# Gated attention and low-rank mixer on one core: the 64-row output tile on four array quadrants, the low-rank step and the burst order moved

## The chip, the cores and the metric

The kernel runs on one core of one Trainium2 chip. The metric is the time of one execution in microseconds (us) on the device, as the median of several runs; less is better. Verdicts are given at 2%: "faster" needs a ratio below 0.98.

Five engines matter. PE is TensorE, the matrix unit; PEld is its loading of weights; ACT is ScalarE; DVE is VectorE; POOL and SP mostly issue DMAs. Each has its own list of instructions in the program and waits for the others by semaphores (counters that one engine raises and another waits on); in the timelines below each works through its list in order.

## The reference

Eight batches, 3136 rows, 256 columns, keys of 64 columns:

```python
scores = (1 / S) * z @ z.T          # S = 3136, z: S x 64
attn   = maximum(scores, 0) ** 2
x      = u * (attn @ v)             # u, v: S x 256

h   = x.T @ U @ V                   # U: S x 32, V: 32 x S   (low rank)
y   = x + h.T
out = y + maximum(y @ w1, 0) @ w2   # w1: 256 x 1024, w2: 1024 x 256
```

## The kernel before

The 3136 rows make 25 tiles: 24 of 128 rows and one of 64 rows (tile `NF = 24`). For each batch the kernel computes 25 *outputs*, one row tile of `attn @ v` each, in the order 12, 13, ..., 24, 0, ..., 11. I number them 0 to 24 in that order, so the 64-row tile is output 12. Into the attention of batch b it weaves the mixer of batch b-1: a *rank* step after output 0 (`x.T @ U`), a *low-rank* step in seven outputs (one for each chunk of up to four tiles), and *bursts* of first-layer steps ("up") and second-layer steps ("down") after outputs 2, 4, 6, 8, 10, 13, 15, 17. It also fills in *scores* (z times z) for its own later outputs and for the next batch.

Each attention matmul takes 64 of 128 rows of the contraction, so two of them run side by side in the two row halves of the array, into two banks of PSUM, the memory that takes TensorE's sums; the pair of banks is summed when two outputs are done (`close_pair`). There are two sets of two banks. One accumulates; the other, `spare()`, serves the low-rank step and the second layer, once the pair before has been summed out of it.

Three inputs of the matmuls are transposed by DMA ("turned"): `zT` (z for the scores), a *strip* (blocks of attn) and `ut` (a chunk of x + h.T for the first layer). A score passes from PE to ACT (L273, the maximum) and to DVE (L275, the square).

```python
def attend_steps(b, o):                  # 25 steps of one output
    def step(i):
        ...
        if i < NT - 1:
            w = block(b, o, js[i])       # 128 x 128 block of attn
            half(b, o, js[i], 0, w, ...) # rows 0..63   -> bank 0
            half(b, o, js[i], 1, w, ...) # rows 64..127 -> bank 1
        ...
        if i == NT - 1 and o == last:
            close_pair(b, o)

def close_pair(b, o):
    nc.scalar.copy(out=both[:, :w], in_=banks[1][:, :w])                   # L347 ACT
    nc.vector.tensor_tensor(both[:, :w], banks[0][:, :w], both[:, :w], add)  # L348 DVE
    nc.vector.tensor_tensor(x_at(b, t0, n), both, u_sb, mult)              # L351 DVE

def low_rank(b, c, ps=None):
    ps = spare() if ps is None else ps
    for ...: mm(out=ps[h][...], lhsT=V_bf[...], rhs=t1[b][...])            # L421 PE
    for h in range(2):
        nc.vector.tensor_tensor(q, ps[h], q, add)                          # L435 DVE
    transpose(out=ut, in_=x)                                               # DMA, for the up steps

# the loop over outputs
main = attend_steps(b, o)
if b and i in ahead:                       # outputs 1, 2, 4, 6, 8, 10, 13
    main.insert(NT * 2 // 5, low_rank step)   # step 10 of 25
_spread(main, fill)                        # fill: score steps, evenly spread
...
run(_merge(down, up))                      # the burst; a down step also takes spare()
```

The 64-row output costs as many matmuls as any other: its rows are doubled into both halves of the 128 weight columns, and half of what comes out is a copy.

Of the kernel before, what the change touches and what calls it, by code (L numbers as in the profile page):

```python
# [10 lines left out]
ALU = mybir.AluOpType  # L11
# [3 lines left out]
def _ceil_div(a, b):  # L15
    return (a + b - 1) // b
# [15 lines left out]
def _merge(*lists):  # L32

    keyed = [
        ((i + 0.5) / len(part), n, s)
        for n, part in enumerate(lists)
        for i, s in enumerate(part)
    ]
    return [s for _, _, s in sorted(keyed, key=lambda e: e[:2])]
# [3 lines left out]
def kernel(  # L43
# [11 lines left out]
    nc = tc.nc  # L55

    B, S, D = u.shape
# [4 lines left out]
    NT = _ceil_div(S, P)  # L62
    NF = S // P
# [31 lines left out]
    halves = [slice(h * ROWS, (h + 1) * ROWS) for h in range(2)]  # L95
# [12 lines left out]
    mm = nc.tensor.matmul  # L108
# [9 lines left out]
    v_both = [persist.tile([P, NT, D], BF16, name=f"v{k}") for k in range(2)]  # L118
# [30 lines left out]
    def x_at(b, t, n=1):  # L149

        c, k = offset[t]
        return group(b, c)[:, :, k : k + n, :].rearrange("p a t c -> p t a c")

    def split(ap):
        return ap.rearrange("p (t a c) -> p t a c", a=ND, c=P)
# [148 lines left out]
    acc = {}  # L304
    u_tiles = {}

    def pair_of(o):
        first = 0 if o < FIRST else FIRST
        stop = FIRST if o < FIRST else NT
        t0 = o - (o - first) % 2  # L310
        return t0, min(2, stop - t0)
# [11 lines left out]
    def open_pair(b, o):  # L323
        acc[pair_of(o)[0]] = sets[opened[0] % 2]
        opened[0] += 1

    def block(b, o, j):
        k = (o - j) % NT
        return A[j][:, k * P : (k + 1) * P] if k <= HALF else strips[b, o][:, NT - 1 - k, :]

    def half(b, o, j, h, w, start, stop, **kw):
        t0, _ = pair_of(o)
        mm(  # L333
            out=acc[t0][h][:, (o - t0) * D : (o - t0 + 1) * D],
            lhsT=w[halves[h]],
            rhs=v_both[b % 2][halves[h], j, :],
            start=start,
            stop=stop,
            **kw,
        )  # L340

    def close_pair(b, o):
        t0, n = pair_of(o)
        banks, u_sb = acc.pop(t0), u_tiles.pop((b, t0))
        w = n * D
        both = both_pool.tile([P, 512], FP32, name="both")
        nc.scalar.copy(out=both[:, :w], in_=banks[1][:, :w])  # L347
        nc.vector.tensor_tensor(  # L348
            out=both[:, :w], in0=banks[0][:, :w], in1=both[:, :w], op=ALU.add
        )  # L350
        nc.vector.tensor_tensor(  # L351
            out=x_at(b, t0, n),
            in0=split(both[:, :w]),
            in1=u_sb[:, :n, :].rearrange("p t (a c) -> p t a c", c=P),
            op=ALU.mult,
        )

    def after(b, o):

        t0, n = pair_of(o)  # L360
        i = place(t0) + n
        return (b, turns(i)) if i < NT else (b + 1, turns(0))

    def attend_steps(b, o):
        t0, n = pair_of(o)
        last = t0 + n - 1
        js = [(o - k) % NT if k < NB else (o + k - HALF) % NT for k in range(NT)]
        js.remove(NF)

        def step(i):  # L370
            if i == 0 and o == t0:
                open_pair(b, o)
                if after(b, o)[0] < B:
                    load_u(*after(b, o))
            if i < NT - 1:
                w = block(b, o, js[i])
                end = i == NT - 2
                half(b, o, js[i], 0, w, i == 0, end and o > t0)
                half(b, o, js[i], 1, w, i == 0 and o == t0, end)
            elif o == t0:  # L380
                half(b, o, NF, 0, block(b, o, NF), False, True)
                if o < last:
                    half(b, o + 1, NF, 1, block(b, o + 1, NF), True, False)
            if i == NT - 1 and o == last:
                close_pair(b, o)

        return [lambda i=i: step(i) for i in range(NT)]
# [26 lines left out]
    def low_rank(b, c, ps=None):  # L414

        ts = chunks[c]
        ps = spare() if ps is None else ps
        where = [(0, 0), (1, 0)] if len(ts) == 2 else [(0, 0), (0, 1), (1, 0), (1, 1)]
        order = sorted(zip(where, ts), key=lambda e: (e[0][1], e[0][0]))
        for (h, k), t in order:  # L420
            mm(  # L421
                out=ps[h][:, k * D : (k + 1) * D],
                lhsT=V_bf[halves[h], col(t) : col(t) + P],
                rhs=t1[b][halves[h], :],
                start=True,
                stop=True,
            )
        n = len(ts)
        x = group(b, c)
        dst = x.rearrange("p a t c -> p t a c")  # L430
        for h in range(2):
            ks = [k for (g, k), _ in zip(where, ts) if g == h]
            k0 = len(ks) * h if n == 2 else 2 * h
            q = dst[:, k0 : k0 + len(ks)]
            nc.vector.tensor_tensor(out=q, in0=split(ps[h][:, : len(ks) * D]), in1=q, op=ALU.add)  # L435
        ut = ut_pool.tile([P, ND * 512], BF16, name="ut")
        ut = ut[:, : ND * n * P].rearrange("p (a w) -> p a w", a=ND)
        transpose(
            out=ut.rearrange("p a (t c) -> p (a t) c", c=P),
            in_=x.rearrange("p a t c -> p (a t c)"),  # L440
        )
        uT[c] = ut
# [211 lines left out]
    own_at = {i: [] for i in range(NT)}  # L654
    for i, j in enumerate(range(LEAD + NG - 1, NT)):
        own_at[i].append((j, 0, NB))
    for j, i in enumerate((6, 7, 8, 9, 10, 10, 4, 2, 9, 8, 7, 6)):
        own_at[i].append((j, 0, FIRST - j))


# [11 lines left out]
    def run(steps):  # L672
        for s in steps:
            s()
# [5 lines left out]
    for b in range(B):  # L680
        more = b + 1 < B
        begin = 0 if b else 2 * NG
        bursts = bursts_of(b - 1) if b else []
        burst_at = dict(zip((2, 4, 6, 8, 10, 13, 15, 17), range(NC + 1)))
        z_load, z_double, z_half, z_turn = (1, 5, 7, 11) if b else (None, 9, 11, 13)
        soon = next_at if b else next_first
        v_at = (1, 3, 4, 5, 7, 8, 10, 11, 12) if b else (8, 9, 10, 12, 14, 15, 16, 17, 18)
        v_at = dict(zip(v_at, V_PARTS))
        ahead = dict(zip((1, 2, 4, 6, 8, 10, 13), range(NC)))
        first = []  # L690
        if b == 0:
            for j, k1 in [(NT - 1, NB)] + [(j, NB if j < 3 else FIRST - j) for j in range(FIRST)]:
                first += score_steps(j, 0, k1)
        for i in range(begin, NT):
            o = turns(i)
            fill = []
            if b == 0:
                if i < z_turn:
                    n = _ceil_div(len(first), z_turn - i)
                    fill, first = first[:n], first[n:]  # L700
            else:
                fill = [s for key in own_at[i] for s in score_steps(*key)]
            if more:
                fill += [s for key in soon[i] for s in score_steps(*key)]
                if i == z_load:
                    load_z(b + 1, WHOLE)
                if i == z_double:
                    double_z(b + 1, WHOLE)
                if i == z_half:
                    turn_z(b + 1, ((FIRST, NF),))  # L710
                if i == z_turn:
                    turn_z(b + 1, ((0, FIRST),))
                if i == z_turn + 1:
                    extend_z()
                if i in v_at:
                    load_v(b + 1, v_at[i])
            main = attend_steps(b, o)
            if b and i in ahead:
                main.insert(NT * 2 // 5, lambda c=ahead[i]: low_rank(b - 1, c))
            _spread(main, fill)  # L720
            if i + AHEAD < NT:
                turn(b, turns(i + AHEAD))
            elif more:
                turn(b + 1, turns(i + AHEAD - NT))
            if b == 0 and i in weights:
                weights[i]()
            if b and i == 0:
                rank(b - 1)
            if b and i in burst_at:
                up, down = bursts[burst_at[i]]  # L730
                if not more and burst_at[i] >= NC - 1:
                    late += up + (down if burst_at[i] == NC else [])
                    up, down = [], (down if burst_at[i] < NC else [])
                run(_merge(down, up))


    last = bursts_of(B - 1)
# [5 lines left out]
    for c in range(NC + 1):  # L743
        up, down = last[c]
        if c + 2 < NC:
            up = up[:1] + [lambda c=c: low_rank(B - 1, c + 2, other)] + up[1:]
# [30 lines left out]
```

## Time and profile before

| | before |
|---|---|
| median of three runs | 1065.91 us (1064.72 to 1067.03) |
| PE busy | 1010.7 us, 95% |
| repeat, batches 2 to 5 | 126.8 us |
| attention matmul, start to start | 54.6 ns (two side by side) |
| output 12 (49 attention matmuls) | 2.68 us |

The page's first part, and the first lines of its part on the chain that ended last (shares of the span):

```profile
PE 1010.7 (95%) x13829; PEld 791.3 (74%) x13829; DVE 525.3 (49%) x937; ACT 611.4 (57%) x814; POOL 178.7 (17%) x332
...
PE 81%; DVE 7%; ACT 5%; issue 3%; DMA 2%; POOL 1%; SPq 0%; POOLq 0%; ACTq 0%; DVEq 0%
```

TensorE bounds this kernel. "Busy", though, hides short waits: the page counts a matmul busy from its start to a modelled end some 270 ns later, and in a stream the next starts 55 ns later. The Trainium skill ("Perfetto Trace Analysis", Tensor Engine Instruction) says the same: the start is taken when the operands are fetched, the end is computed. So I measure a wait on PE by starts: how much later a matmul starts than its stream's rate allows. By that measure output 4's low-rank matmul below is 0.58 us late; by the page's idle column it is 0.37.

The chain in order of time shows each batch's rank step; the columns are start, length, and what. The differences between such lines are the repeats:

```profile
496.98 1.53 PE ps L401 x50
623.82 1.53 PE ps L401 x50
```

The view of waits (who waited for whom: us in total, times, longest), three lines:

```profile
PE ps L260 <- DMA zT<-z_bf: 15.8, 2, 9.6
PE ps L421 <- DVE both L348: 8.3, 28, 0.4
PE ps L333 <- DVE x_bf L435: 2.3, 7, 0.3
```

The two waits for zT are in the start-up and in batch 0. The 28 of L421 are four in each of seven batches, at outputs 4, 6, 8 and 10. The timeline of output 4 (columns: start, length, engine, line, what, count, idle before) shows one:

```profile
513.35 0.58 ACT L347 COPY both<-ps 128x512 f32<-128x512 f32 x1
513.99 0.68 DVE L348 TENSOR_TENSOR both<-ps,both 128x512 f32<-128x512 f32 x1
514.73 0.40 PE L421 MATMUL ps<-t_sb,V_bf 64*128 64x256 bf16 x4 [0.37 <-DVE both L348]
515.82 1.28 DVE L435 TENSOR_TENSOR x_bf<-ps,x_bf 128x512 bf16<-128x512 f32 x2
517.16 0.38 PE L486 MATMUL ps<-w_bf,relu 128*128 128x256 bf16 x2
```

PE comes to the low-rank step while DVE still sums the pair before out of the same banks (L348 ends at 514.67). The burst then begins with a second-layer step (L486) at 517.16, just after the low-rank adds L435 have left its bank (515.82 + 1.28 = 517.10).

Output 12 in the timeline, its first 24 and the next 24 of 49 matmuls:

```profile
566.49 1.47 PE L333 MATMUL ps<-v,A 64*128 64x256 bf16 x24
567.80 1.47 PE L333 MATMUL ps<-v,strip 64*128 64x256 bf16 x24
```

567.80 - 566.49 = 1.31 us for 24 starts, 54.6 ns each.

### The profile page before, as it was taken

How to read it: one execution, taken by the hardware profiler on the slowest of the kernel's cores; microseconds unless marked ns; L12 is line 12 of the kernel's file. 1: busy time of each engine (PE TensorE's matmuls, PEld its weight loads, DVE VectorE, ACT ScalarE, POOL GpSimd, SP SyncE). 2: the span in 40 equal slices, each digit the busy share in tenths (PEclk: the TensorE clock that was granted, in tenths of full speed). 3: DMA queues.
4: the chain of work that ended last, by engine and by line, in shares of the span. 5: the costliest groups of instructions: out<-in, count | busy, mean ns of one | idle time of the engine just before them, and what ended most of it. 6: DMA issues, size and time to landing. Idle time of an engine off the chain costs nothing.

```text
span 1063.6 us, 31097 instructions
## 1 busy us (share of the span) xinstructions
PE 1010.7 (95%) x13829; PEld 791.3 (74%) x13829; DVE 525.3 (49%) x937; ACT 611.4 (57%) x814; POOL 178.7 (17%) x332
## 2 busy tenths in 40 slices
PE   5879999999999999999999999999899999999896
PEld 4667777787777867788677877788677787778564
DVE  4858554465544654456543555436444465432331
ACT  5857555566645665466655665646665566541253
POOL 4122112111121111211121121211112110111011
PEclk9999999999999999999999999999999999999998
DMA  9999989779897998959899898987989797588231
GB/s 173 183 195 179 174 165 173 168 159 171 167 164 158 174 173 170 179 139 163 162 174 178 152 170 163 165 183 145 173 155 172 158 170 136 125 149 162 62 100 64
DMA packets 417174, 168.71 MB, mean 159 GB/s; under 512 B 392768, under 2 KB 402640, under 8 KB 417040
## 3 DMA queue, kind: packets, MB, share of 16 engines
q1 hardware_dynamic: 386464, 96.77, 56.9%
q0 software_dynamic: 30576, 69.96, 27.1%
q8 instruction: 108, 1.77, 0.7%
q14 instruction: 26, 0.21, 0.1%
HBM read 61.88 MB, written 25.69 MB: 82 GB/s over the span
## 4 chain that ended last, share of the span: by engine, by line
PE 81%; DVE 7%; ACT 5%; issue 3%; DMA 2%; POOL 1%; SPq 0%; POOLq 0%; ACTq 0%; DVEq 0%
PE ps L333 43%; PE ps L486 16%; PE ps L455 15%; PE ps L260 6%; ACT A L273 3%; DVE x_bf L435 3%; DVE both L348 2%; DVE A L275 2%; DMA zT<-z_bf 1%; PE ps L401 1%; DVE x_bf L351 1%; ACT both L347 1%; PE ps L421 1%; ACT relu L462 1%; DMA ut<-x_bf 1%
## 5 line engine op out<-in xcount | busy, mean ns | idle before, releaser
L273 ACT ACTIVATE A<-ps 128x832 bf16<-128x832 f32 (+8 forms) x469 | 351.7, 763 | 176.4 <-PE ps L260 170.6
L333 PE MATMUL ps<-v,A 64*128 64x256 bf16 x5064 | 358.6, 271 | 5.7 <-DVE x_bf L435 2.3
L275 DVE TENSOR_TENSOR A<-A 128x832 bf16<-128x832 bf16 (+8 forms) x469 | 240.3, 524 | 209.8 <-ACT A L273 206.8
L333 PE MATMUL ps<-v,strip 64*128 64x256 bf16 x4612 | 319.9, 270 | 0.0
L462 ACT ACTIVATE relu<-ps 128x1024 bf16<-128x1024 f32 (+2 forms) x224 | 203.1, 916 | 186.0 <-PE ps L455 186.0
L333 PEld LDWEIGHTS <-A 64*128 64x128 bf16 x5064 | 251.7, 94 | 64.5 <-issue 27.1
L333 PEld LDWEIGHTS <-strip 64*128 64x128 bf16 x4612 | 233.2, 94 | 34.1 <-issue 0.2
L455 PE MATMUL ps<-ut,w_bf 128*128 128x512 bf16 (+2 forms) x896 | 204.4, 354 | 7.4 <-DMA ut<-x_bf 4.3
L486 PE MATMUL ps<-w_bf,relu 128*128 128x256 bf16 x1600 | 205.9, 273 | 1.0
L486 PEld LDWEIGHTS <-relu 128*128 128x128 bf16 x1600 | 153.8, 98 | 49.5 <-issue 9.3
L497 DVE TENSOR_TENSOR o_sb<-ps,x_bf 128x512 f32<-128x512 f32 (+1 forms) x104 | 69.7, 670 | 221.3 <-PE ps L486 221.3
L260 PE MATMUL ps<-zT 64*128 64x416 bf16 (+9 forms) x933 | 156.0, 318 | 18.4 <-DMA zT<-z_bf 15.8
L455 PEld LDWEIGHTS <-w_bf 128*128 128x128 bf16 x896 | 86.3, 98 | 65.6 <-issue 11.6
L317 POOL DMA_DIRECT2D u_sb<-in_u_dram x96 | 53.5, 558 | 474.4 <-DVE x_bf L351 436.0
L504 POOL DMA_DIRECT2D out_dram<-o_sb x96 | 52.4, 546 | 330.2 <-DVE o_sb L497 330.2
L348 DVE TENSOR_TENSOR both<-ps,both 128x512 f32<-128x512 f32 (+1 forms) x104 | 69.3, 666 | 55.4 <-ACT both L347 55.0
L347 ACT COPY both<-ps 128x512 f32<-128x512 f32 (+1 forms) x104 | 58.9, 567 | 63.0 <-PE ps L333 63.0
L260 PEld LDWEIGHTS <-zT 64*128 64x128 bf16 x933 | 53.0, 95 | 27.2 <-DMA zT<-z_bf 16.1
L435 DVE TENSOR_TENSOR x_bf<-ps,x_bf 128x512 bf16<-128x512 f32 (+1 forms) x112 | 65.4, 626 | 14.7 <-PE ps L421 14.6
L351 DVE TENSOR_TENSOR x_bf<-both,u_sb 128x512 bf16<-128x512 f32 (+1 forms) x104 | 69.8, 671 | 3.6
L195 POOL DMA_DIRECT2D v<-in_v_dram x61 | 34.1, 566 | 0.5 <-issue 0.5
L421 PE MATMUL ps<-t_sb,V_bf 64*128 64x256 bf16 x200 | 22.6, 273 | 9.9 <-DVE both L348 8.3
(33 smaller groups left out, 134.0 us busy)
## 6 DMA issues: line engine op xcount, KB each, us to landing
u_sb<-in_u_dram POOLq DMA_DIRECT2D x96, 256.0 KB, 3.5
out_dram<-o_sb POOLq DMA_DIRECT2D x96, 256.0 KB, 3.0
v<-in_v_dram POOLq DMA_DIRECT2D x57, 192.0 KB, 5.7
strip<-A SPq DMA_TRANSPOSE x196, 4.9
z_c<-in_z_dram POOLq DMA_DIRECT2D x7, 384.0 KB, 5.7
w_bf<-in_moe_w_ch_dram POOLq DMA_DIRECT2D x2, 512.0 KB, 8.5
u_sb<-in_u_dram POOLq DMA_DIRECT2D x16, 64.0 KB, 2.1
ut<-x_bf SPq DMA_TRANSPOSE x56, 3.4
```

The costliest lines, as they stand in the source:

```text
L260: mm(out=ps[:, k, :n], lhsT=zT[halves[k], j, :], rhs=zT_flat[halves[k], c : c + n], start=True, stop=True,)
L273: nc.scalar.activation(out=dst, in_=src, func=AF.Relu, scale=sc)
L275: nc.vector.tensor_tensor(out=dst, in0=dst, in1=dst, op=ALU.mult)
L333: mm(out=acc[t0][h][:, (o - t0) * D : (o - t0 + 1) * D], lhsT=w[halves[h]], rhs=v_both[b % 2][halves[h], j, :], start=start, stop=stop, **kw,)
L347: nc.scalar.copy(out=both[:, :w], in_=banks[1][:, :w])
L348: nc.vector.tensor_tensor(out=both[:, :w], in0=banks[0][:, :w], in1=both[:, :w], op=ALU.add)
L351: nc.vector.tensor_tensor(out=x_at(b, t0, n), in0=split(both[:, :w]), in1=u_sb[:, :n, :].rearrange("p t (a c) -> p t a c", c=P), op=ALU.mult,)
L435: nc.vector.tensor_tensor(out=q, in0=split(ps[h][:, : len(ks) * D]), in1=q, op=ALU.add)
L455: mm(out=ps[:, i, :w], lhsT=w1_bf[:, db, (hp + i) * P : (hp + i + 1) * P], rhs=uT[c][:, db, len(chunks[c]) * P - w :], start=(db == 0), st ...
L462: nc.scalar.activation(out=relus[c][:, hp : hp + 2, :w], in_=ps[:, :, :w], func=AF.Relu)
L486: mm(out=ps[:, k * D : (k + 1) * D], lhsT=relus[c][:, ht, q : q + P], rhs=w2_bf[:, ht, :], start=(ht == 0), stop=(ht == NH - 1),)
L497: nc.vector.tensor_tensor(out=o_sb[:p, :nk, :].rearrange("p t (a c) -> p t a c", c=P), in0=split(ps[:p, : nk * D]), in1=x_at(b, t, nk)[:p] ...
```

## The change

Its intent: compute the 64-row output with 64 weight columns instead of 128, so that four 64x64 quadrants of the array work at once; take the low-rank step later, when the pair sum is done; hide the low-rank adds behind a first-layer step; and turn the second half of the next z one output sooner, for which two score groups move from output 10 to outputs 3 and 5.

```diff
 def close_pair(b, o):
     ...
+        if o == NF:
+            for r in range(2):
+                nc.scalar.copy(out=both[halves[r], w : 2 * w], in_=both[halves[1 - r], :w])
+            nc.vector.tensor_tensor(
+                out=both[:, :w], in0=both[:, :w], in1=both[:, w : 2 * w], op=ALU.add
+            )
 ...
+    def quarter(b, j, n, h):
+        c = n % 2
+        mm(
+            out=acc[NF][h][halves[c], :D],
+            lhsT=block(b, NF, j)[halves[h], halves[c]],
+            rhs=v_both[b % 2][halves[h], j, :],
+            start=(n < 2),
+            stop=(n == (NT - 2 if c else NT - 1 - 2 * h)),
+        )
 ...                                        # in attend_steps
+            if o == NF:
+                if i < NT - 1 and i % 2:
+                    for n in (i - 1, i):
+                        for h in range(2):
+                            quarter(b, js[n], n, h)
+                elif i == NT - 1:
+                    quarter(b, NF, i, 0)
 ...
-    for j, i in enumerate((6, 7, 8, 9, 10, 10, 4, 2, 9, 8, 7, 6)):
+    for j, i in enumerate((6, 7, 8, 9, 3, 5, 4, 2, 9, 8, 7, 6)):
 ...
-        z_load, z_double, z_half, z_turn = (1, 5, 7, 11) if b else (None, 9, 11, 13)
+        z_load, z_double, z_half, z_turn = (1, 5, 7, 10) if b else (None, 9, 11, 13)
 ...
-                main.insert(NT * 2 // 5, lambda c=ahead[i]: low_rank(b - 1, c))
+                main.insert(8 if i == 1 else 14, lambda c=ahead[i]: low_rank(b - 1, c))
 ...
-                run(_merge(down, up))
+                run(_merge(up, down))
```

The added lines shift the numbers. In the changed kernel the low-rank matmul is L445 (L421 before), its adds L459 (L435), the first layer L479 (L455), the second layer L510 (L486), the rank step L425 (L401), the product with u L357 (L351); L333, L347 and L348 keep theirs, the quadrants are L367, the copies between halves L353 and their sum L354.

More of the change, by code (lines that the diff above doesn't have):

```diff
@@ L374, in step @@
                     load_u(*after(b, o))
-            if i < NT - 1:
+            if o == NF:
[5 more added lines that the diff above has]
+                    quarter(b, NF, i, 0)
+            elif i < NT - 1:
                 w = block(b, o, js[i])
```

## The prediction

> **What bounds it now.** TensorE. The page has PE busy 1010.7 of 1063.6 us; 81% of the chain that ended last is PE. Batches 1 to 7 repeat every 126.8 us (rank bursts of L401 in the chain, 496.98 and 623.82). The timeline shows attention matmuls (two 64-row halves side by side) starting every 54.6 ns (24 in 1.31 us), the 128-row matmuls of 256 columns about every 109 ns. Summing instructions at their rates leaves only about 5 us of a batch for stalls and switches:
> - low-rank matmuls waiting for the pair sum: at outputs 4, 6, 8, 10 of a batch, starts 0.58, 0.60, 0.39, 0.47 us late (L421 waits for DVE L348), 2.0 us a batch;
> - output 2 opening on banks that the low-rank adds L435 hold: 0.54 us;
> - the all-first-layer burst waiting for ACT relu: 0.47 us;
> - entering and leaving bursts: 0.15 to 0.29 and 0.10 us.
>
> **Step 1, quadrants (8 times).** The 64-row output costs 49 matmuls, 49 x 54.6 = 2.68 us. The count stays 49; the question is whether four run at once. L401 already runs four column groups with different data at 27 ns a start, so I take 27 ns: 1.34 us, less two array switches at the 0.15 us which L333 to L401 shows: net 1.0 us. The Trainium skill ("TensorEngine Tiling (Array Packing)", Key Properties) says tiles load and multiply in parallel and that changing the mode drains; its Restrictions say column tiling disables fast weight load. This trace agrees about the switch (0.15 us) and, for 32-column loads, about concurrency; 64-column loads are not in it: that is the risk. In batches 1 to 7 no score falls into this output, so it stays one run. In batch 0 three scores interrupt it and PE afterwards waits 6.2 us for zT's DMA, so little is gained there. The cross-half copies and the add (about 0.4 us each) sit on ACT and DVE, off the path. Worth 7 to 8 us.
>
> **Step 2, low-rank at step 14.** Four steps and a score give 0.44 + 0.17 us, so the wait should shrink. Two things give part of it back. Output 3 and 5 get one more score, which delays their pair copy on ACT, hence L348, by about 0.3 us: remaining waits 0.2 to 0.3 us at outputs 4, 6 and 10. And the instruction order shows that the low-rank adds now queue on DVE behind the second score's square; I place their end 4.4 to 5.1 us into the output, after the burst's start (3.5 to 3.9 us). The first-layer step in front (0.86 us) hides most of that, leaving 0 to 0.5 us before the first second-layer matmul. Net 0.3 to 1 us a batch, 2 to 7 us. At output 1, moving to step 8 changes no order on DVE (the adds still follow the first square), so 0.54 us stays.
>
> **Step 3, z sooner.** PE waits for zT only at start-up and in batch 0, neither changed; nothing of itself, it only keeps z ahead of a faster PE.
>
> **Sum:** 1065.9 - 7.5 - 5 = about 1053 us (ratio 0.988). Range 1045 to 1061. Chances: faster by over 2% 0.13, within 2% 0.86, slower 0.01.
>
> **What would show it.** Right: the quadrant matmuls span about 1.4 us an output, starts 27 to 30 ns apart; period 124.5 to 126 us; waits of L421 for L348 fall from 8.3 us to under 4; new waits of the second-layer matmul for the low-rank add. Wrong: quadrant starts still near 54 ns (weight loads bind: 1060 or more); no new second-layer waits and L421's gone (then 1046 or less); the wait for ut that batch 6 shows once (1.9 us), coming in more batches since the DMA engines are 89% busy.

## The result

| | before | after |
|---|---|---|
| median | 1066.2 us (4 runs) | 1057.22 us (4 runs, 1054.92 to 1058.27) |
| ratio | | 0.9914, 95% interval 0.9894 to 0.9934 |
| repeat, batches 2 to 4 | 126.83 us | 125.47 us |
| first rank step | 116.06 us | 118.07 us |
| span of the profiled run | 1063.6 us | 1055.1 us |

The output was correct. The gain of 0.9% is clear of noise.

The page, the chain, the waits and the two stretches of the timeline, as above, of the changed kernel:

```profile
PE 1005.0 (95%) x13829; PEld 776.9 (74%) x13829; DVE 527.6 (50%) x945; ACT 617.9 (59%) x830; POOL 178.7 (17%) x332
```

```profile
494.86 1.53 PE ps L425 x50
620.32 1.53 PE ps L425 x50
```

```profile
PE ps L260 <- DMA zT<-z_bf: 17.8, 2, 9.7
PE ps L510 <- DVE x_bf L459: 3.2, 14, 0.3
PE ps L333 <- DVE x_bf L459: 2.3, 7, 0.3
PE ps L445 <- DVE both L348: 1.7, 7, 0.2
```

The wait of the low-rank matmul for the pair sum has shrunk, and a new one has come: the second-layer matmul L510 waits for the low-rank add.

```profile
511.82 0.58 ACT L347 COPY both<-ps 128x512 f32<-128x512 f32 x1
511.96 0.69 DVE L275 TENSOR_TENSOR A<-A 128x1024 bf16<-128x1024 bf16 x1 [0.66 <-ACT A L273]
512.57 0.68 DVE L348 TENSOR_TENSOR both<-ps,both 128x512 f32<-128x512 f32 x1
513.30 0.39 PE L445 MATMUL ps<-t_sb,V_bf 64*128 64x256 bf16 x4 [0.24 <-DVE both L348]
513.89 1.08 DVE L275 TENSOR_TENSOR A<-A 128x832 bf16<-128x832 bf16 x2
514.90 1.28 DVE L459 TENSOR_TENSOR x_bf<-ps,x_bf 128x512 bf16<-128x512 f32 x2
514.99 1.04 PE L479 MATMUL ps<-ut,w_bf 128*128 128x512 bf16 x4
516.23 1.03 PE L510 MATMUL ps<-w_bf,relu 128*128 128x256 bf16 x8 [0.20 <-DVE x_bf L459]
```

This is output 4 again. The square of the 1024-wide score that was moved into output 3 now stands on DVE just ahead of L348. The low-rank matmuls end at 513.69, but both squares of this output's scores (L275, x2) stand ahead of the adds L459, which end only at 516.18, and L510 starts right after.

```profile
564.18 0.85 PE L367 MATMUL ps<-v,A 64*64 64x256 bf16 x24
564.86 0.82 PE L367 MATMUL ps<-v,strip 64*64 64x256 bf16 x24
565.71 0.94 PE L333 MATMUL ps<-v,A 64*128 64x256 bf16 x14
```

The quadrants do what was hoped: 24 starts in 0.68 us, and 49 starts at 27.8 ns on average; single starts come 3, 4, 3 and 99 ns apart.

Adding up one batch, by starts, against before:

- the quadrants: before, 49 x 54.6 ns = 2.68 us; after, 1.53 us from the first quadrant's start to the next attention matmul (565.71 - 564.18), and 0.14 us for the switch of the array mode ahead of it (where the tile shape changes, the first quadrant starts 0.199 us after the matmul before it and not 0.055): 1.0 us gained;
- late low-rank matmuls at outputs 4, 6, 8, 10: 0.58, 0.60, 0.39, 0.47 us became 0.45, 0.31, 0, 0.25: 1.03 us gained;
- late second-layer matmuls at outputs 4, 6, 8: 0.37, 0.18, 0.42 us are new: 0.97 lost, against 0.27 that two burst entries lost before for the same reason.

Together 1.33 us; the repeat fell by 1.36. Of the 8.5 us between the two profiled spans, seven batches at 1.36 give 9.5. Another 1.2 us is luck of these two executions: before had, in its batch 6, a rare wait of 1.87 us for ut, and after had one of 0.69, in its batch 5 (0.15 of each is the mode switch). The start took 2.0 us longer, and the end 0.3.

### The profile page after: what moved, and what is told of

The parts are those of the page before. It is cut to its first block, busy times and chain, and to the rows that moved or that the text cites. A ratio compares the mean times of both kernels' runs of the same rounds, so it can differ in the third digit from the quotient of the medians.

```text
span 1055.1 us, 31120 instructions
## 1 busy us (share of the span) xinstructions
PE 1005.0 (95%) x13829; PEld 776.9 (74%) x13829; DVE 527.6 (50%) x945; ACT 617.9 (59%) x830; POOL 178.7 (17%) x332
## 4 chain that ended last, share of the span: by engine, by line
PE 80%; DVE 7%; ACT 4%; DMA 4%; issue 3%; POOL 1%; SPq 0%; POOLq 0%; ACTq 0%; DVEq 0%
PE ps L333 41%; PE ps L510 16%; PE ps L479 14%; PE ps L260 5%; ACT A L273 3%; DVE x_bf L459 3%; DVE A L275 2%; DVE both L348 2%; DMA zT<-z_bf 1%; PE ps L367 1%; PE ps L425 1%; DVE x_bf L357 1%; PE ps L445 1%; ACT relu L486 1%; DMA v<-in_v_dram 1%
## 5 line engine op out<-in xcount | busy, mean ns | idle before, releaser
L333 PE MATMUL ps<-v,A 64*128 64x256 bf16 x4864 | 332.0, 271 | 5.5 <-DVE x_bf L459 2.3
L275 DVE TENSOR_TENSOR A<-A 128x832 bf16<-128x832 bf16 (+8 forms) x469 | 240.5, 523 | 180.0 <-ACT A L273 177.7
L333 PE MATMUL ps<-v,strip 64*128 64x256 bf16 x4420 | 312.5, 270 | 0.0
L486 ACT ACTIVATE relu<-ps 128x1024 bf16<-128x1024 f32 (+2 forms) x224 | 203.3, 917 | 177.7 <-PE ps L479 177.7
L333 PEld LDWEIGHTS <-A 64*128 64x128 bf16 x4864 | 235.4, 95 | 60.1 <-issue 24.2
L333 PEld LDWEIGHTS <-strip 64*128 64x128 bf16 x4420 | 221.5, 94 | 34.6 <-issue 0.2
L479 PE MATMUL ps<-ut,w_bf 128*128 128x512 bf16 (+2 forms) x896 | 205.1, 355 | 6.2 <-DMA ut<-x_bf 3.2
L510 PE MATMUL ps<-w_bf,relu 128*128 128x256 bf16 x1600 | 205.7, 273 | 3.4 <-DVE x_bf L459 3.2
L510 PEld LDWEIGHTS <-relu 128*128 128x128 bf16 x1600 | 155.4, 98 | 54.2 <-issue 10.8
L260 PE MATMUL ps<-zT 64*128 64x416 bf16 (+10 forms) x933 | 154.3, 319 | 20.1 <-DMA zT<-z_bf 17.8
L479 PEld LDWEIGHTS <-w_bf 128*128 128x128 bf16 x896 | 83.6, 98 | 71.0 <-issue 18.6
L348 DVE TENSOR_TENSOR both<-ps,both 128x512 f32<-128x512 f32 (+1 forms) x104 | 69.2, 665 | 47.4 <-ACT both L347 47.0
L347 ACT COPY both<-ps 128x512 f32<-128x512 f32 (+1 forms) x104 | 58.8, 566 | 54.5 <-PE ps L333 48.4
L459 DVE TENSOR_TENSOR x_bf<-ps,x_bf 128x512 bf16<-128x512 f32 (+1 forms) x112 | 65.4, 625 | 15.0 <-PE ps L445 15.0
L357 DVE TENSOR_TENSOR x_bf<-both,u_sb 128x512 bf16<-128x512 f32 (+1 forms) x104 | 69.8, 671 | 3.6
L445 PE MATMUL ps<-t_sb,V_bf 64*128 64x256 bf16 x200 | 21.8, 273 | 4.1 <-DVE both L348 1.7
```

What stands on the lines that cost most here:

```text
L260: mm(out=ps[:, k, :n], lhsT=zT[halves[k], j, :], rhs=zT_flat[halves[k], c : c + n], start=True, stop=True,)
L275: nc.vector.tensor_tensor(out=dst, in0=dst, in1=dst, op=ALU.mult)
L333: mm(out=acc[t0][h][:, (o - t0) * D : (o - t0 + 1) * D], lhsT=w[halves[h]], rhs=v_both[b % 2][halves[h], j, :], start=start, stop=stop, **kw,)
L348: nc.vector.tensor_tensor(out=both[:, :w], in0=banks[0][:, :w], in1=both[:, :w], op=ALU.add)
L357: nc.vector.tensor_tensor(out=x_at(b, t0, n), in0=split(both[:, :w]), in1=u_sb[:, :n, :].rearrange("p t (a c) -> p t a c", c=P), op=ALU.mult,)
L459: nc.vector.tensor_tensor(out=q, in0=split(ps[h][:, : len(ks) * D]), in1=q, op=ALU.add)
```

## The experiments

All were correct. Ratios are to the kernel before. Repeats are differences of rank-step starts in the chain, from the batches without a rare DMA wait (the third to fourth rank step, unless said).

| run | median us | ratio (95% interval) | repeat us |
|---|---|---|---|
| before | 1065.8 to 1066.35 | | 126.83 |
| after | 1057.22 | 0.9914 (0.9894 to 0.9934) | 125.47 |
| e1_quads | 1064.96 | 0.9992 (0.9977 to 1.0008) | 126.75 |
| e2_step14 | 1071.53 | 1.0059 (1.0037 to 1.0082) | 127.83 (fifth to sixth) |
| e3_step14_up | 1056.04 | 0.9903 (0.9888 to 0.9918) | 125.55 |
| e4_z_late | 1050.39 | 0.9853 (0.9838 to 0.9868) | 124.60 |
| e5_quads_c6_late | 1058.9 | 0.9934 (0.9919 to 0.9949) | 125.74 |
| e6_adds_first | 1044.53 | 0.9808 (0.9791 to 0.9824) | 123.97 |
| e7_first_sooner | 1041.41 | 0.9767 (0.9750 to 0.9784) | 123.40 |
| e8_start | 1052.38 | 0.9860 (0.9814 to 0.9905) | 123.39 |
| e9_start_less | 1039.55 | 0.9755 (0.9735 to 0.9776) | 123.41 |
| e10_burst3 | 1040.29 | 0.9754 (0.9731 to 0.9777) | 123.28 |

My theory was that step 2 of the change (step 14 and burst order) trades one wait for another, since the add stands behind a score's square on DVE, and that the two moved scores cost what little is left. The rivals: the quadrants give little and the low-rank step most; the moved scores are free; z is needed sooner.

### e1_quads: the quadrants alone

```diff
 # of the changed kernel, undone: both tuples, and
-main.insert(8 if i == 1 else 14, ...)
+main.insert(NT * 2 // 5, ...)
-run(_merge(up, down))
+run(_merge(down, up))
```

> The kernel before with the quadrant output alone (low-rank at step 10, second-layer step first, z and scores as before). Theory: the quadrants are the larger part of the gain: one run of 49 starts of 27.8 ns plus two switches of about 0.15 us against 2.68 us, so 1.04 us less in each of batches 1 to 7: repeat of 125.8 us, total about 7 us under the kernel before (ratio 0.993), batch 0 aside, whose wait for zT's DMA may move by 2 us either way. Rival: the gain of the change comes from the low-rank step, and the quadrants give half of that or less (repeat of 126.3 us or more).

Measured: repeat 126.75 us, ratio 0.9992. My expectation missed: alone, the quadrants gain next to nothing. They run at the same 27.8 ns, so the loss is elsewhere. At output 13, right after them, the low-rank matmul is 0.39 us late and the second-layer matmul 0.81 (with the mode switch of 0.15 in it), neither of which was late before. Part of the timeline there, DVE and ACT first, then PE:

```profile
568.90 0.55 DVE L189 COPY zT<-zT 128x1536 bf16<-128x1536 bf16 x1
569.36 0.42 DVE L348 TENSOR_TENSOR both<-ps,both 128x256 f32<-128x256 f32 x1
569.82 0.82 ACT L353 COPY both<-both 64x256 f32<-64x256 f32 x2 [1.06 <-DVE both L348]
570.67 0.43 DVE L354 TENSOR_TENSOR both<-both 128x256 f32<-128x256 f32 x1 [0.88 <-ACT both L353]
571.60 0.75 DVE L459 TENSOR_TENSOR x_bf<-ps,x_bf 128x256 bf16<-128x256 f32 x2
...
569.84 0.29 PE L445 MATMUL ps<-t_sb,V_bf 64*128 64x256 bf16 x2 [0.17 <-DVE both L348]
572.41 0.81 PE L510 MATMUL ps<-w_bf,relu 128*128 128x256 bf16 x6 [0.59 <-DVE x_bf L459]
```

The copy that extends zT (L189) stands ahead of the pair sum L348. Then DVE sits idle 0.88 us while ACT copies between the halves, and the low-rank add queues behind all of it. In the changed kernel the same chain is there, but with step 14 and a first-layer step in front of the second layer nobody waits for it. So at this one output the quadrants need the other two edits.

### e5_quads_c6_late: the same, with that one low-rank step an output later

```diff
-ahead = dict(zip((1, 2, 4, 6, 8, 10, 13), range(NC)))
+ahead = dict(zip((1, 2, 4, 6, 8, 10, 14), range(NC)))
```

> The quadrants alone, as in e1_quads, but the low-rank sums of the last chunk moved from output 13 to output 14. In e1_quads the quadrants ran as fast as in the changed kernel (27.8 ns a start), but output 13 lost 0.39 us (L445 for the pair sum) and about 0.8 us (second-layer matmul for the low-rank add), because the longer closing of the 64-row output stands in front of the low-rank add on DVE. Theory: away from that output the chain of copies is off the path and the saving of 1.04 us comes back: repeat 125.7 to 125.9 us (e1_quads 126.75, before 126.83), ratio 0.993. Rival (the quadrants need step 14 and the burst order for another reason): repeat stays at 126.5 us or more.

Measured: repeat 125.74 us, ratio 0.9934, as the theory had it. The saving comes back when the low-rank step is taken away from output 13. The 0.39 and 0.81 us are gone from the trace, while the four waits at outputs 4, 6, 8 and 10 stay as in the kernel before. The later low-rank step was not run without the quadrants; but nothing was late at output 13 in the kernel before, so by its trace there was nothing for it to gain.

### e2_step14 and e3_step14_up: the low-rank step moved, without and with the burst order

```diff
-main.insert(NT * 2 // 5, ...)
+main.insert(8 if i == 1 else 14, ...)
 # e3 only:
-run(_merge(down, up))
+run(_merge(up, down))
```

> The kernel before with only the low-rank sums moved (step 14; step 8 at output 1), the second-layer step still first in a burst. Theory: the wait of L421 for DVE L348 nearly vanishes (2.0 us a batch to about 0.1), but the low-rank adds now stand on DVE behind the second score's square, and the first second-layer matmul of the burst waits for them: 0.8 to 1.3 us at outputs 4, 6, 8 and 10. Net 1 to 1.5 us more a batch: repeat of 127.8 to 128.3 us, ratio 1.007 to 1.010. Rival: the wait is the cost, so removing it gains its 2 us a batch (repeat 124.8 us, ratio 0.987).

> As the run before, and the first-layer step first in a burst; z and the two scores as in the kernel before. Theory: the first-layer step (0.86 us; 0.54 at output 8) hides most of the wait for the adds; and as outputs 3 and 5 carry no extra score, the pair sum is not later, so L421 waits about 0.1 us a batch in all, against 1.0 in the changed kernel: repeat about 125.4 us (1.4 under before), ratio about 0.990. Rival (the two moved scores cost nothing): the step-14 part is worth what it is worth in the changed kernel, 0.3 us a batch: repeat 126.5 us.

Measured: e2 has a repeat of 127.83 us, 1.0 us more than before, though the wait it was meant to remove is gone. In its waits, the line of L421 for L348 no longer shows, and this one is new:

```profile
PE ps L486 <- DVE x_bf L435: 20.7, 21, 1.1
```

Two lines of output 4's timeline in e2:

```profile
519.30 1.28 DVE L435 TENSOR_TENSOR x_bf<-ps,x_bf 128x512 bf16<-128x512 f32 x2
520.63 0.60 PE L486 MATMUL ps<-w_bf,relu 128*128 128x256 bf16 x4 [1.11 <-DVE x_bf L435]
```

By starts L486 is 1.32, 1.15 and 1.13 us late at outputs 4, 6 and 8 (0.15 of each is the mode switch). At output 10 I had expected a wait as well, and none shows; that is why e2 lost 0.6% and not 0.7 to 1.0%.

e3 puts the first-layer step in front and falls to 125.55 us (expected 125.4): 1.28 us under before, with nothing left of the low-rank wait and 0.30, 0.13 and 0.43 us of the second-layer wait at outputs 4, 6 and 8. In the changed kernel the same two edits were worth 0.36 us (1.36 less the quadrants' 1.0). What that kernel has besides is the moved scores and z, which the next run takes out together (z alone was not run).

### e4_z_late: the changed kernel with z and the two scores as before

```diff
-for j, i in enumerate((6, 7, 8, 9, 3, 5, 4, 2, 9, 8, 7, 6)):
+for j, i in enumerate((6, 7, 8, 9, 10, 10, 4, 2, 9, 8, 7, 6)):
-z_load, z_double, z_half, z_turn = (1, 5, 7, 10) if b else ...
+z_load, z_double, z_half, z_turn = (1, 5, 7, 11) if b else ...
```

> The changed kernel with the second half of z turned at output 11 again and the two scores back at output 10. Theory: turning z sooner buys nothing in batches 1 to 7 (no wait for zT there), and the two scores that it moved to outputs 3 and 5 delay the pair sum by about 0.3 us there; undone, the waits of L445 for L348 at outputs 4 and 6 (0.45 and 0.31 us) fall to 0.1 or less: repeat about 124.4 us against 125.46 in the changed kernel, total about 7 us less than it (ratio to before 0.985). Rival: z is needed sooner once the quadrants shorten output 12; then a wait for zT of 0.5 us or more shows at output 13 of the batches and the repeat is 125.5 us or more.

Measured: repeat 124.60 us, ratio 0.9853, 7 us better than the changed kernel. No wait for zT appears in batches 1 to 7. The wait of L445 for L348 has left the list of waits; by starts, no low-rank matmul of the batch that I went through start by start is as much as 0.1 us late, and the sum over its seven is 0.85 us less than in the changed kernel, which is nearly all of the 0.87 us. So this part of the change is a loss. Output 4 in e4, where the low-rank matmul starts 0.11 us after the two matmuls before it:

```profile
508.37 0.27 PE L333 MATMUL ps<-v,strip 64*128 64x256 bf16 x2
508.48 0.38 PE L445 MATMUL ps<-t_sb,V_bf 64*128 64x256 bf16 x4
```

At outputs 4 and 6 it follows from one queue: in the changed kernel the extra score's ACT pass and its square on DVE come before the pair's copy and sum at the end of outputs 3 and 5, as the lines of output 4 above show. At output 10 (0.2 of the 0.85 us) it is another thing: there the pair sum ends 1.7 us into the output in both kernels, but in the changed one no score stands ahead of the low-rank matmul any more, and PE comes to it sooner.

### e6_adds_first: the adds ahead of the second score's square

```diff
 # e4_z_late, and
-_spread(main, fill)
+if b and i in ahead and len(fill) == 3:       # outputs 2, 4, 6, 8
+    for k, at in enumerate((5, 17, 23)):      # scores after steps 5, 17 and 23; low-rank stays at 14
+        main.insert(at + k, fill[k])
+    run(main)
+else:
+    _spread(main, fill)
```

> e4_z_late (repeat 124.60 us) with the second and third score of outputs 2, 4, 6 and 8 put after the low-rank step, which stays at step 14, so that its adds stand on DVE in front of the second score's square. Theory: the remaining waits of the second-layer matmul for the add (0.30 and 0.43 us at outputs 4 and 8) are due to that order; they go to under 0.15 us: repeat 124.0 to 124.2 us, ratio to before 0.981 to 0.982. Rival (DVE is simply too busy there, the order is not it): the waits stay within 0.1 us and the repeat at 124.6 us.

Measured: repeat 123.97 us, ratio 0.9808. The second-layer waits at outputs 4, 6 and 8 are gone, with no work removed from DVE: only its order changed. (The low-rank matmuls are 0.15 and 0.16 us late at outputs 4 and 6 again, as no second score comes in front of them now.) From output 4's timeline:

```profile
508.77 0.39 PE L445 MATMUL ps<-t_sb,V_bf 64*128 64x256 bf16 x4
509.36 0.58 DVE L275 TENSOR_TENSOR A<-A 128x832 bf16<-128x832 bf16 x1
509.86 1.28 DVE L459 TENSOR_TENSOR x_bf<-ps,x_bf 128x512 bf16<-128x512 f32 x2
510.63 1.04 PE L479 MATMUL ps<-ut,w_bf 128*128 128x512 bf16 x4
511.06 1.05 DVE L275 TENSOR_TENSOR A<-A 128x832 bf16<-128x832 bf16 x2
```

One square ahead of the adds instead of two; they end at 511.14, before the second layer wants the bank at about 511.5. The Trainium skill ("TensorE: Matmul & The Clock Gate", Architectural detail) says that ACT and DVE work strictly first in, first out; e6 agrees: with one square less ahead of them the adds end 2.37 us after the low-rank matmul's start, against 2.88 in the changed kernel.

### e7_first_sooner: the first chunk's low-rank step ahead of the first score

```diff
-main.insert(8 if i == 1 else 14, ...)
+main.insert(6 if i == 1 else 14, ...)
```

> e6_adds_first with the first chunk's low-rank step at step 6 of output 1, in front of the first score, in place of step 8, behind it. Theory: step 8 changed nothing (0.54 us at the opening of output 2 in before, after and e4 alike) because the adds stood behind the first score's square on DVE; in front of it the 0.54 us go: repeat 0.5 us under e6, about 123.6 us, ratio about 0.977. Rival: the adds are late because the rank sums come late; then the wait only shrinks by the two steps, 0.2 us.

Measured: repeat 123.40 us in the one undisturbed batch, 123.7 to 123.8 in four and 124.5 in one, ratio 0.9767. The 0.54 us at the opening of output 2, which step 8 had left untouched in the changed kernel, are gone. In most batches 0.4 us or so come back: in the one that I went through start by start, the burst after output 2 waits 0.37 us for ut, as the output now ends before the transpose lands. With 1041.41 us e7 beats both kernels and is faster than before by over 2%.

### e8_start, e9_start_less and e10_burst3: what else is left

> e7_first_sooner with batch 0 alone changed: the next batch's v is loaded at outputs 15 to 23 in place of 8 to 18, and z is doubled and its first half turned one output sooner. Aim: the wait of PE for zT in batch 0 (6.2 us in before, 8.1 us in the changed kernel), the largest single wait left. Theory: the transposes are slow there (7 to 11 us from issue to landing against 4 to 5 later) because the v loads share the DMA engines; without them the wait falls to about 3 us, and the total by 3 to 5 us; repeats unchanged. Rival: the transposes limit each other, and the wait stays at 6 us or more.

> e7_first_sooner with a milder version of e8_start: in batch 0 the first three v loads stay at outputs 8 to 10 and the other six go to outputs 15 to 20 (18 in e7, 23 in e8). In e8 the wait for zT fell from about 8 to 2.9 us as expected, but v and a strip came late at the end of batch 0 and cost 7 us. Theory: with v ready three outputs sooner the loss at the end is gone and 3 us or more of the gain stay: about 1038 us, ratio about 0.974. Rival: the DMA engines are full for the whole of batch 0, so whatever is taken from one place is lost at another: 1041 us or more.

> e7_first_sooner with the first burst, which has first-layer steps alone, after output 3 in place of output 2. In e7 0.52 us (0.15 of it the array switch) stand in front of that burst in one batch: the transpose ut arrives late, since output 2 now begins 0.54 us sooner. Theory: an output later it has landed, so the 0.37 us go and with them the rare wait of about 1 us: repeats of 123.0 us in all of batches 1 to 6, ratio about 0.974. Rival: the two bursts in a row (outputs 3 and 4) make ACT or DVE late, and the repeat grows.

```diff
 # e8, against e7 (batch 0 only)
-z ... (None, 9, 11, 13)      v_at ... (8, 9, 10, 12, 14, 15, 16, 17, 18)
+z ... (None, 8, 10, 13)      v_at ... (15, 16, 17, 18, 19, 20, 21, 22, 23)
 # e9, against e7
+z ... (None, 8, 10, 13)      v_at ... (8, 9, 10, 15, 16, 17, 18, 19, 20)
 # e10, against e7
-burst_at = dict(zip((2, 4, 6, 8, 10, 13, 15, 17), ...))
+burst_at = dict(zip((3, 4, 6, 8, 10, 13, 15, 17), ...))
```

e8 cut the wait for zT in batch 0 to 2.6 us, as expected, but its total rose by 11 us in place of falling by 3 to 5. PE then waited 6.8 us for strips and a little for v at the end of batch 0, and 3.7 us for ut in batch 1, which lasted 130.49 us against 123.70 in e7. The moved v loads and the transposes seem to have got in each other's way there: strips issued 95 to 118 us into e8 took 9.5 to 18.5 us to land, against 3.7 to 5.8 in that stretch of e7. And a long wait costs more than its length, as the last wait for a strip and the rank step right after it show:

```profile
121.64 0.39 PE L333 MATMUL ps<-v,strip 64*128 64x256 bf16 x1 [5.97 <-DMA strip<-A]
121.96 2.96 PE L425 MATMUL ps<-x_bf,U_bf 128*32 128x256 bf16 x50
```

The groups of four matmuls in this rank step start 0.21 us apart in place of 0.11, and after the wait for ut the first-layer matmuls start 0.427 us apart in place of 0.213; the granted clock from 119 to 130 us was 0.69. (The profile is of the slowest of four executions, which spread from 1043.1 to 1054.87 us.) e9 kept the end clean but left the zT wait at 7.0 us, so taking away the loads at outputs 12 and 14 did not shorten it; whether those at 8 to 10 slow the transpose, or the sooner first half in company with them, stays open. Its 1039.55 us cannot be told from e7's. e10's repeats are 123.28 or 123.29 us in four batches in a row and 123.56 in the sixth, as the wait for ut is gone; I had expected 123.0. Its whole time cannot be told from e7's either, as the intervals overlap.

## Why the prediction was right

The time (1057.22 us against 1053, range 1045 to 1061) and the class were right, and so was nearly every step; of the 12.5 us forecast, 9.0 came. Point by point:

- **Quadrants.** Predicted 27 ns a start and 1.0 us a batch; measured 27.8 ns and 1.0. The risk that I named, 64-column weight loads, did not bind. "Off the path" was right in the changed kernel only: e1 shows that the copies and the add cost the whole gain when the low-rank step stands close behind them, and e5 that with this step an output later the gain is there again. The prediction did not see this: that the other two edits came with the quadrants was luck.
- **Low-rank step.** Predicted: remaining waits of 0.2 to 0.3 us at outputs 4, 6, 10, and 0 to 0.5 us of new second-layer waits, net 0.3 to 1 us a batch. Measured: 0.45, 0.31, 0.25; new 0.37, 0.18, 0.42; net 0.36, the low end. The sum of 5 us for this term was too large: 7 x 0.36 = 2.5 us. e2 and e3 show the trade itself, e6 its cause.
- **Output 1 at step 8.** Predicted no effect; the 0.54 us stayed, and e7 shows why.
- **z sooner.** Predicted to be worth nothing of itself. It was worth less than nothing: together with the scores it moved it cost 0.87 us a batch (e4). The text had counted that delay inside step 2, at about 0.3 us at each of two outputs.
- **Batch 0.** Predicted "little is gained there"; in the profiled run 2.0 us were lost, with a wait for zT of 8.1 us in place of 6.2. The windows of both kernels (columns: window, length, busy time and count of each engine in the order PE, PEld, DVE, ACT, POOL, then granted clock, DMA share, GB/s), first before, then after:

```profile
72.00:84.00 12.00, 5.76 (x68) 4.02 (x65) 3.55 (x7) 2.21 (x5) 1.38 (x2) 0.73 1.24 214
84.00:119.00 35.00, 35.00 (x632) 28.77 (x630) 26.56 (x46) 25.51 (x36) 7.58 (x13) 1.00 1.00 181
```

```profile
72.00:84.00 12.00, 3.92 (x56) 2.86 (x52) 2.48 (x4) 1.25 (x3) 0.46 (x2) 0.67 1.19 197
84.00:119.00 35.00, 35.00 (x612) 28.29 (x611) 27.64 (x50) 25.79 (x35) 7.57 (x14) 0.97 0.99 179
```

  The lower clocks of after, 0.67 and 0.97, do not mean a slower stretch: in both kernels the matmuls start half as often for 5 us after the wait (pairs of attention matmuls 0.213 us apart in place of 0.109; granted clock 0.51 before from 79.4 to 84.4 us, 0.52 after from 81.5 to 86.5), and the edge at 84 us cuts this stretch at another place. By starts the wait lasts 6.51 us in before and 8.35 in after, and from its end to the first rank step it is 36.6 us in both. So the wait itself is 1.84 of the 2.0 us. Ahead of it, after lost 0.7 us by output 12, with a granted clock of 0.67 between 30 and 35 us where before had 1.00, and won 0.4 of it back with the quadrants. That clock is scatter: from 20 to 40 us it is 1.00 in e5, 0.91 in after and 0.83 in e7, which have one and the same batch 0. The wait is another matter: it lasts 6.2 to 6.5 us in the three profiles without quadrants (before, e2, e3) and 6.6 to 8.35 in the seven with quadrants and the same batch 0 (after, e1, e4, e5, e6, e7, e10), so the quadrants seem to lengthen it; why was not tested.

## What to carry to other kernels

When a wait is on a buffer, moving the waiting step later helps only if everything that the step feeds stays early: look up where its consumer stands in the in-order queue of the next engine, since one score's square ahead of it gave most of the gain back here, and changing that order alone returned it. A saving on the bounding engine counts only after its added side work has found a place away from the next user of the same buffers and queues; test the saving alone as well as in company, because here it was worth 0.1 us or 1.0 us a batch depending on its neighbours. And compare steady repeats from the trace, not only whole times: effects of 0.3 us a batch showed there to 0.05 us while whole times scatter by 3 us; leave out the batches with a rare wait.

## What the Trainium skill lacked or had wrong

- "TensorEngine Tiling (Array Packing)", Key Properties, says that changing the mode drains the engine, but not what it costs. Here, by starts beyond the stream's rate: 0.144 to 0.147 us from two 64x128 tiles into 64x64, 128x32 or 128x128, about 0.10 us from 128x128 back; and from 64x64 back the next matmul starts 0.20 us after the last quadrant's start.
- The same page, Restrictions, says that column tiling turns fast weight load off, but not whether that binds. The loads of 64x64 took 106 ns on average against 94 for 64x128, and four quadrants still ran at 27.8 ns a start over 256 columns.
- "TensorE: Matmul & The Clock Gate", Part 3, gives packed tiles about 4 ns of start distance each. The runs agree inside a group (3, 4, 3 ns) and add what it does not say of groups in a row: the next one starts 99 ns later, so a group of four takes 109 ns, the time of one matmul, and the 4 ns are not added.
- "TensorEngine Tiling (Array Packing)", PSUM Bottleneck, warns that the copy out of PSUM may bind after tiling. It does not say that two added copies and an add for one half-sized tile may cost as much as the tile saves while DVE is only half busy, when the next user of the banks is near (e1: 0.08 us a batch gained in place of 1.0).
